# Keeping all row sums for one check at the end, with a second program behind a branch

## The chip, the cores and the metric

The kernel runs on one core of a Trainium2 chip. The metric is the device time of one execution in microseconds. The runs of the kernel before gave 521.4, 522.92 and 527.8 us; their median is 522.92 us.

## The reference

Attention whose heads are mixed before and after the softmax ("talking heads"), followed by a feed-forward block with a squared ReLU. The inputs q, k, v and both mixing matrices are normal draws times 0.1.

```python
batch, n_heads, seq, head_dim = (8, 12, 448, 64)
n_tokens, d_model, d_ff = (3584, 768, 2048)

scores = scale * np.matmul(q, k.transpose(0, 1, 3, 2))        # scale = 1/8
scores = np.einsum('bhij,hg->bgij', scores, w_pre)
scores = scores - np.max(scores, axis=-1, keepdims=True)
attn = np.exp(scores)
attn = attn / (np.sum(attn, axis=-1, keepdims=True) + 1e-09)
attn = np.einsum('bhij,hg->bgij', attn, w_post)
x = np.matmul(attn, v)                                        # to (3584, 768)
h = np.maximum(x @ w_in, 0.0)
out = h * h @ w_out
```

## The kernel before

For each of the 8 batches the 448 queries are cut into 45 chunks of 10 queries (the last has 8), so that 10 queries times 12 heads fill the 128 partitions of a tile, with 4 padding rows in each half. The names of the steps are those of the streams in the code:

- `T` transposes q and k, `QK` (L894) makes the scores of one head, which are copied to `stage` and moved by DMA (`rel`, issued by SyncE, L940) into `dring`, where the 12 heads of a chunk lie side by side on the partitions.
- `pre` (L963) mixes the heads by a matmul. In batch 0 the first 22 chunks go another way (`dir`, L842): there the mix is multiplied into q.
- `exp` (L980, ScalarE) writes the exponential of a chunk to `pring` and, with `accum_out`, its row sums to `rowsum`, a ring of 10 slots. No maximum is subtracted. `rec` (L994, VectorE) takes the reciprocal of the sums of two chunks, and `fold` (L1001, mostly GpSimd) multiplies it into the second mixing matrix, `wk2s`.
- `post` (L1033) mixes the heads again and gives the transposed attention, copied to `a2t` (the `a2ev` tasks, L459 on ScalarE and L460 on VectorE). `AV` (L1092) multiplies by v into `xt`.
- `F1` (L1138, L1159) and `F2` (L1279) are the feed-forward block: ReLU into `h1t` (L1190 on ScalarE, L1191 on VectorE), square into `h2t` (L1200, VectorE), output copied to `osb` and stored, from GpSimd's queue (L1311). The last two tiles of the last batch go through `emit_last` (L1228), and are stored from the queues of SyncE and ScalarE (L1251).

The order of the work is made when the program is built. TensorE's order is written out by hand, in the string `ORDER`, one digit for each unit of a stream. A planner (`_Plan`) walks through it with a cost for every task and puts the tasks of the other engines into lists: each engine runs its list strictly in order and waits on semaphores. Copies out of PSUM carry the engine `FLEX`: the planner gives each to ScalarE or VectorE, whichever would be done earlier by its costs. So a task added on one engine can move a copy to the other one.

```python
def fn_exp(eng, en):                                            # L979
    return eng.activation(pring[:, pr, 0:S], ps[:, gr.banks[x], 0:S], AF.Exp,
                          accum_out=rowsum[:, pr, :])
def fn_rec(eng, en):                                            # L993
    return eng.reciprocal(rinv[:, p0:p0 + n, :], rowsum[:, p0:p0 + n, :])
def fn_final(eng, en):                                          # L1381
    for s in sem_out + [sem_last]:
        eng.wait_ge(s.handle, s.count)
```

At the end SyncE's last task, `final`, waits until all outputs have landed; then every engine branches to a common closing block with a barrier over all five.

Of the kernel before, what the change touches and what calls it, by code (L numbers as in the profile page):

```python
# [7 lines left out]
ALU = mybir.AluOpType  # L8
# [3 lines left out]
PE = "pe"  # L12
# [306 lines left out]
def bass_talking_heads_attention__then__ffn_squared_relu_kernel(  # L319
# [43 lines left out]
    with ExitStack() as es:  # L363
# [14 lines left out]
        WARM = 60000  # L378
        WSHARE = 0.6
# [30 lines left out]
        zrow = sb("zrow", [128, S], DT.bfloat16)  # L410
# [19 lines left out]
        sem_last = Sm("olast")  # L430
        sem_out = [Sm("oslot%d" % i) for i in range(NOS)]

        plan = _Plan(NB)

        def c_pe(t):
            return {PE: (t, t + 190.0)}

        def c_ev(cols):
            return {ACT: (cols / 1.2 + 65.0, cols / 1.2 + 175.0),
                    DVE: (cols / 0.96 + 72.0, cols / 0.96 + 160.0)}  # L440

        def add(name, engine, fn, deps, cost, prio, mode=None, group=None, instrs=0):
            return plan.add(name, engine, fn, deps, cost, prio, "ctr", 1, mode, group=group,
                            instrs=instrs)

        events = {}

        def unit(s, name, fn, deps, ns, mode, group, mms):
            kind = name[:2]
            was = events.get(kind, 0.0)  # L450
            events[kind] = was + EVENTS.get(kind, 0.5)
            n = 2 * mms + int(events[kind]) - int(was)
            t = add(name, PE, fn, deps, c_pe(ns), 0, mode, group, n)
            s.append(t)
            return t

        def copy(eng, en, o, i_):
            if en == ACT:
                return eng.activation(o, i_, AF.Copy)  # L459
            return eng.tensor_copy(o, i_)  # L460

        streams = [[] for _ in range(10)]
        plan.streams = streams
        s_T, s_QK, s_pre, s_post, s_AV, s_dir = streams[:6]
        s_F1, s_F2 = streams[6:8], streams[8:]
# [3 lines left out]
        def fn_init(eng, en):  # L469
            eng.memset(mask[:, :, :], 1.0)  # L470
            eng.memset(wk1[:, :], 0.0)
            eng.memset(wrep[:, :], 0.0)
            eng.memset(wk2b[:, :, :], 0.0)
            return eng.memset(ident[:, :], 0.0)

        t_init = add("init", DVE, fn_init, [], {DVE: (750.0, 850.0)}, -3e6)

        def fn_init2(eng, en):
            return eng.affine_select(ident[:, :], ident[:, :], pattern=[[-1, 128]],
                                     compare_op=ALU.not_equal, fill=1.0, base=0,  # L480
                                     channel_multiplier=1)

        t_init2 = add("init2", POOL, fn_init2, [t_init], {POOL: (310.0, 430.0)}, -1e7 + 1)

        def select(name, m, pattern, base, mult, deps, prio):
            def fn(eng, en):
                return eng.affine_select(m[:, :, :], m[:, :, :], pattern=pattern,
                                         compare_op=ALU.is_ge, fill=0.0, base=base,
                                         channel_multiplier=mult)

            return add(name, POOL, fn, deps, {POOL: (150.0, 250.0)}, prio)

        def halves(name, m, deps, prio):
            def fn(eng, en):
                return eng.tensor_tensor(m[:, 0, :], m[:, 0, :], m[:, 1, :], ALU.add)

            return add(name, DVE, fn, deps, {DVE: (80.0, 160.0)}, prio)

        t_m = select("init3", mask, [[-PR, 2], [-H, H5]], -R0, 1, [t_init], -1e7 + 20)
        t_m = select("init4", mask, [[PR, 2], [H, H5]], R0 + H - 1, -1, [t_m], -1e7 + 21)  # L500
        t_mask = halves("init5", mask, [t_m], -461.0)

        def fn_mask2(eng, en):
            r_ = None
            for x in range(2):
                i_ = ident[64 * x:64 * x + 64, 64 * x:64 * x + PR].rearrange(
                    "p (b a) -> p a b", a=H5)
                r_ = eng.tensor_reduce(mask2[64 * x:64 * x + 64, :], i_, AX.X, ALU.add)
            return r_

        t_mask2 = add("init8", DVE, fn_mask2, [t_init2], {DVE: (330.0, 410.0)}, -460.0)

        def fn_zero(eng, en):
            return eng.memset(vraw[64:128, :, NS - 1, :], 0.0)

        t_zero = [add("zero", DVE, fn_zero, [], {DVE: (300.0, 400.0)}, -3e6 + 1)]
        t_z = []
        t_zrow = add("zrow", DVE, lambda eng, en: eng.memset(zrow[0:R0, :], 0.0), [],
                     {DVE: (300.0, 400.0)}, -3e6 + 2)

        def fn_zdma(eng, en):
            eng.dma_start(dring[0:R0, :, :], zrow[0:R0, :].unsqueeze(1).to_broadcast(
                [R0, NDS, S])).then_inc(sem_z.handle, 16)

        def fn_wsmall(eng, en):
            src = bass.AP(w_pre.tensor, 0, [[0, CH], [H, H], [1, H]])
            eng.dma_start(wrep[R0:R0 + NR, :], src).then_inc(sem_w0.handle, 16)
            for x in range(2):
                src = bass.AP(w_post.tensor, 0, [[H, H], [0, H5], [1, H]])
                eng.dma_start(wrep2[64 * x:64 * x + PR, :], src).then_inc(sem_w0.handle, 16)  # L530
            return None

        def fn_wall(eng, en):
            src = bass.AP(w_pre.tensor, 0, [[0, 128], [1, H * H]])
            eng.dma_start(wall[:, :, :, :].rearrange("p a b c -> p (a b c)"), src).then_inc(
                sem_wq.handle, 16)
            return None

        t_wall = plan.add("wall", SP, fn_wall, [], {SP: (400.0, 5300.0)}, -1e6 - 1, sem_wq, 16)
        wq_of = []  # L540
        for kk in range(2):
            def fn_wq(eng, en, r0=kk * 64, kk=kk):
                r_ = None
                for u in range(2):
                    i_ = wall[r0:r0 + 64, kk:NP:2, u, :].unsqueeze(3).to_broadcast([64, 3, H, H5])
                    r_ = eng.tensor_scalar(wq[r0:r0 + 64, 3 * u:3 * u + 3, :, :], i_,
                                           scale, None, op0=ALU.mult)
                return r_

            wq_of.append(add("wq%d" % kk, DVE, fn_wq, [t_wall], {DVE: (560.0, 640.0)}, -2e6))  # L550

        def fn_wk1(eng, en):
            o = wk1[:, 0:PR].rearrange("p (b a) -> p b a", a=H5)
            i0 = wrep[:, :].unsqueeze(2).to_broadcast([128, H, H5])
            i1 = mask[:, 0, :].unsqueeze(1).to_broadcast([128, H, H5])
            return eng.scalar_tensor_tensor(o, i0, scale, i1, op0=ALU.mult, op1=ALU.mult)

        def fn_wk2(eng, en):
            r_ = None
            for x in range(2):  # L560
                r0, r1 = 64 * x, 64 * x + PR
                i0 = wrep2[r0:r1, :].unsqueeze(2).to_broadcast([PR, H, H5])
                i1 = mask2[r0:r1, :].unsqueeze(1).to_broadcast([PR, H, H5])
                r_ = eng.tensor_tensor(wk2b[r0:r1, :, :], i0, i1, ALU.mult)
            return r_

        t_warm = add("warm", DVE, lambda eng, en: eng.memset(warm[:, :], 0.5), [],
                     {DVE: (600.0, 700.0)}, -4e6)

        def warm_up(gap):  # L570
            now = plan.free[PE]
            if now > WARM or not t_warm.done:
                return
            n = int((gap - 100.0) * (0.42 if now < 6000.0 else WSHARE) / 190.0)
            if n < 1 or plan.find(1, now)[0] > now + gap:
                return
            g = _Group(1)

            def fn(eng, en):
                r_ = None  # L580
                for _ in range(n):
                    r_ = eng.matmul(ps[0:128, g.banks[0], 0:S], warm[:, 0:128], warm[:, :],
                                    start=True, stop=True)
                return r_

            t = add("warm%d" % len(plan.tasks), PE, fn, [t_warm], c_pe(n * 190.0), 0, "full", g,
                    2 * n)
            t.nwait = 0
            g.readers = [[t]]
            start = max(now, t_warm.end + SEM_LAT, plan.find(1, now)[0])  # L590
            plan._commit_pe(t, start + (MODE_SWITCH if plan.mode != "full" else 0.0))

        plan.warm_up = warm_up

# [877 lines left out]
```

## Time and profile before

| what | value |
|---|---|
| runs, us | 521.4, 522.92, 527.8 |
| profiled execution: span, us | 524.4 |
| instructions in the profile | 23175 |
| TensorE (PE) busy | 510.3 us, 97% |
| ScalarE (ACT) busy | 423.3 us, 81% |
| VectorE (DVE) busy | 394.3 us, 75% |
| GpSimd (POOL) busy | 199.1 us, 38% |
| granted TensorE clock, mean | 0.999 |

The span is the time of the profiled execution from its first to its last instruction; the profile gives no other time of its own for this execution. In the profile's rows, `PE ps L1279` means a matmul of line 1279 that writes PSUM; `SPq` and `ACTq` are DMA issues from the queues of SyncE and ScalarE. In a timeline row stand the start, the time and the engine, and in brackets the idle time before with what ended it. In the table of stretches each engine has its busy time and its number of instructions, and after these come the granted clock, the share of DMA and GB/s.

### The profile page before, as it was taken

How to read it: one execution, taken by the hardware profiler on the slowest of the kernel's cores; microseconds unless marked ns; L12 is line 12 of the kernel's file. 1: busy time of each engine (PE TensorE's matmuls, PEld its weight loads, DVE VectorE, ACT ScalarE, POOL GpSimd, SP SyncE). 2: the span in 40 equal slices, each digit the busy share in tenths (PEclk: the TensorE clock that was granted, in tenths of full speed). 3: DMA queues.
4: the chain of work that ended last, by engine and by line, in shares of the span. 5: the costliest groups of instructions: out<-in, count | busy, mean ns of one | idle time of the engine just before them, and what ended most of it. 6: DMA issues, size and time to landing. Idle time of an engine off the chain costs nothing.

```text
span 524.4 us, 23175 instructions
## 1 busy us (share of the span) xinstructions
PE 510.3 (97%) x9633; PEld 322.6 (62%) x9633; DVE 394.3 (75%) x987; ACT 423.3 (81%) x1218; POOL 199.1 (38%) x391
## 2 busy tenths in 40 slices
PE   7999998999999999999999999999999999999997
PEld 4455766567667565566555665566556565567974
DVE  7965978799888669978998769874788678955430
ACT  3788998989989889888997888988888788786411
POOL 9603454423651365135532456124621333132000
PEclk9999999999999999999999999999999999999999
DMA  9999999746984589646984699547974566541003
GB/s 159 199 215 193 153 195 183 185 90 132 172 177 111 121 183 168 144 89 151 174 159 103 139 182 177 113 90 151 175 113 89 118 154 134 115 101 49 2 22 100
DMA packets 82240, 71.85 MB, mean 137 GB/s; under 512 B 13226, under 2 KB 79514, under 8 KB 82138
## 3 DMA queue, kind: packets, MB, share of 16 engines
q0 software_dynamic: 36624, 32.81, 38.4%
q1 hardware_dynamic: 45226, 37.38, 29.6%
q8 instruction: 77, 1.26, 1.0%
q10 hardware_dynamic: 288, 0.20, 0.1%
q14 instruction: 25, 0.20, 0.1%
HBM read 45.70 MB, written 11.01 MB: 108 GB/s over the span
## 4 chain that ended last, share of the span: by engine, by line
PE 87%; DVE 5%; DMA 4%; ACT 1%; issue 1%; POOL 0%; ACTq 0%; POOLq 0%; DVEq 0%
PE ps L1279 26%; PE ps L1159 18%; PE ps L1033 8%; PE ps L963 7%; PE ps L1138 7%; PE ps L1092 7%; PE ps L894 6%; PE ps L842 5%; DMA dring<-stage 3%; DVE stage L460 2%; PE ps L1228 2%; PE ps L745 2%; DMA kraw<-in_k_dram 2%; DVE a2t L460 1%; ACT pring L980 1%
## 5 line engine op out<-in xcount | busy, mean ns | idle before, releaser
L980 ACT ACTIVATE pring<-ps 128x448 bf16<-128x448 f32 x360 | 191.9, 558 | 17.4 <-PE ps L963 8.7
L1279 PE MATMUL ps<-w_out_sb,h2t 64*128 64x384 bf16 x1664 | 151.8, 323 | 0.7 <-issue 0.6
L1001 POOL TENSOR_TENSOR wk2s<-wk2b,rinv 128x120 bf16<-128x120 bf16 (+1 forms) x179 | 70.7, 398 | 198.6 <-DVE rinv L994 197.8
L460 DVE CAST a2t<-ps 128x480 bf16<-128x480 f32 x194 | 118.6, 640 | 18.9 <-PE ps L1033 17.5
L1159 PE MATMUL ps<-xt,w_in_sb 64*128 64x448 bf16 (+2 forms) x1344 | 122.2, 323 | 1.1 <-issue 1.0
L460 DVE CAST stage<-ps 128x448 bf16<-128x448 f32 (+1 forms) x182 | 109.1, 618 | 11.7 <-PE ps L894 7.7
L1279 PEld LDWEIGHTS ps<-w_out_sb,h2t 64*128 64x128 bf16 x1664 | 77.6, 94 | 51.2 <-issue 4.0
L459 ACT ACTIVATE stage<-ps 128x448 bf16<-128x448 f32 (+1 forms) x178 | 92.2, 558 | 20.2 <-PE ps L894 18.0
L459 ACT ACTIVATE a2t<-ps 128x480 bf16<-128x480 f32 (+1 forms) x174 | 92.5, 577 | 12.6 <-PE ps L1033 11.7
L1159 PEld LDWEIGHTS ps<-xt,w_in_sb 64*128 64x128 bf16 x1344 | 61.4, 94 | 41.9 <-issue 2.5
L980 ACT ACTIVATION_READ_ACCUMULATOR pring<-ps 128x1 f32 x360 | 80.1, 222 | 0.0
L1311 POOL DMA_DIRECT2D out_dram<-osb x52 | 33.7, 653 | 111.1 <-ACT pring L980 62.2
L1033 PEld LDWEIGHTS ps<-wk2s,pring 60*128 60x128 bf16 x2880 | 55.9, 93 | 22.1 <-ACT pring L980 2.5
L1033 PE MATMUL ps<-wk2s,pring 60*128 60x60 bf16 x2880 | 62.3, 187 | 0.4 <-POOL wk2s L1001 0.2
L994 DVE RECIPROCAL rinv<-rowsum 128x2 f32<-128x2 f32 (+1 forms) x184 | 29.1, 158 | 37.1 <-ACT pring L980 36.2
L1200 DVE TENSOR_TENSOR h2t<-h1t 128x448 bf16<-128x448 bf16 (+2 forms) x176 | 52.3, 326 | 6.0 <-ACT h1t L1190 5.7
L1190 ACT ACTIVATE h1t<-ps 128x448 bf16<-128x448 f32 (+2 forms) x91 | 40.1, 451 | 20.6 <-PE ps L1159 15.9
L963 PE MATMUL ps<-dring,wk 64*64 64x448 bf16 (+1 forms) x676 | 52.5, 362 | 2.6 <-DVE rinv L994 1.1
L1191 DVE TENSOR_SCALAR h1t<-ps 128x448 bf16<-128x448 f32 (+2 forms) x85 | 41.7, 496 | 17.0 <-PE ps L1159 9.6
L894 PE MATMUL ps<-qkt 64*128 64x448 bf16 (+1 forms) x360 | 49.4, 354 | 0.2 <-DVE qkt L460 0.2
L1138 PE MATMUL ps<-xt,w_in_sb 128*128 128x220 bf16 (+1 forms) x384 | 41.5, 260 | 1.6 <-ACT stage L459 1.6
L1092 PE MATMUL ps<-a2t,vraw 128*64 128x220 bf16 (+1 forms) x768 | 40.4, 260 | 0.2 <-ACT a2t L459 0.2
(57 smaller groups left out, 416.4 us busy)
## 6 DMA issues: line engine op xcount, KB each, us to landing
dring<-stage SPq DMA_DIRECT2D x309, 105.0 KB
out_dram<-osb POOLq DMA_DIRECT2D x52, 192.0 KB, 3.6
qraw<-in_q_dram POOLq DMA_DIRECT2D x42, 112.0 KB, 5.6
kraw<-in_k_dram POOLq DMA_DIRECT2D x42, 112.0 KB, 5.0
w_in_sb<-in_moe_w_in_dram POOLq DMA_DIRECT2D x8, 384.0 KB, 15.0
vraw<-in_v_dram POOLq DMA_DIRECT2D x24, 128.0 KB
w_out_sb<-in_moe_w_out_dram POOLq DMA_DIRECT2D x8, 384.0 KB, 8.2
vraw<-in_v_dram POOLq DMA_DIRECT2D x24, 96.0 KB
```

Source lines behind the costliest of these rows:

```text
L459: return eng.activation(o, i_, AF.Copy)
L460: return eng.tensor_copy(o, i_)
L894: r_ = eng.matmul(ps[y * w:(y + 1) * w, g.banks[x], 0:S], qkt[r0:r0 + 64, pb, p + y, 0, i0:i0 + w], qkt[r0:r0 + 64, pb, p + y, 1, :], star ...
L963: r_ = eng.matmul(ps[64 * y:64 * y + 64, gr.banks[x], 0:S], wk1[64 * x:64 * x + 64 - R0 * x, :], dring[64 * x:64 * x + 64 - R0 * x, (g0 + ...
L980: return eng.activation(pring[:, pr, 0:S], ps[:, gr.banks[x], 0:S], AF.Exp, accum_out=rowsum[:, pr, :])
L1001: return eng.tensor_tensor(wk2s[:, p0:p0 + n, :], i0.to_broadcast([128, n, PR]), rinv[:, p0:p0 + n, :].to_broadcast([128, n, PR]), ALU.mult)
L1033: r_ = eng.matmul(ps[:, gr.banks[x], o0:o0 + PR], pring[64 * x:64 * x + PR, pr + y, j0:j0 + 2 * PJ], wk2s[64 * x:64 * x + PR, pr + y, :], ...
L1092: r_ = eng.matmul(ps[kk * 64:kk * 64 + 64, g.banks[0], x * n:(x + 1) * n], vraw[:, h, s, :], a2t[half][:, s, h, a0:a0 + n], start=(s == 0) ...
L1138: r_ = eng.matmul(ps[:, g.banks[0], 0:n], w_in_sb[:, ft, t * 128:(t + 1) * 128], xt[:, ft, c0:c1], start=(ft == 0), stop=(ft == NFT - 1))
L1159: r_ = eng.matmul(ps[:, g.banks[x], 0:n], w_in_sb[64 * y:64 * y + 64, ft, t * 128:(t + 1) * 128], xt[64 * y:64 * y + 64, ft, c0:c1], start ...
L1200: return eng.tensor_tensor(h2t[:, t16, o0:o0 + n], h1t[:, s, 0:n], h1t[:, s, 0:n], ALU.mult)
L1279: r_ = eng.matmul(ps[:, g.banks[hh], 0:FH], h2t[64 * y:64 * y + 64, t16, col:col + 128], w_out_sb[64 * y:64 * y + 64, t16, hh * FH:(hh + 1 ...
```

## The change

- The ring `rowsum` is replaced by `sums`, which has a place for every chunk of every batch (8 x 46 places). `exp` writes its sums there and `rec` reads them from there. A small filler buffer is cut so that the later buffers keep their alignment, and the row of zeros `zrow` becomes a part of `osb` (the first copies to `osb` wait for the DMA that reads the zeros).
- After all exponentials four VectorE operations take maximum and minimum of all sums on each partition and compare them with 1e30 and 1e-20; a DMA from SyncE (`row`) puts the 128 answers into one row; two VectorE operations reduce them and write an integer, `flag`.
- Everything that builds tasks is put into a function `program(safe)` and called twice, with one set of semaphores that counts on. The second program, `safe`, subtracts the row maximum: for every chunk a maximum and a negation on VectorE, and a bias at the exponential.
- At the end of its list each engine waits for `flag`, loads it into a register and branches: if it is below 1, it runs its part of the second program. SyncE's last task, `final`, stands behind the branch.
- `ORDER` is the same, and serves both programs.

```diff
+        SUM_MOST = 1e30
+        SUM_LEAST = 1e-20
-        rowsum = sb("rowsum", [128, NPS, 1], DT.float32)
+        sums = sb("sums", [128, B * NCP, 1], DT.float32)
+        nmax = sb("nmax", [128, NPS, 2], DT.float32)
+        test = sb("test", [128, 4], DT.float32)
+        flag = sb("flag", [1, 1], DT.int32)
         rinv = sb("rinv", [128, NPS, 1], DT.float32)
-        sb("align", [128, 64], DT.uint8)
+        sb("align", [128, 16], DT.uint8)
...
-        zrow = sb("zrow", [128, S], DT.bfloat16)
+        zrow = osb.bitcast(DT.bfloat16)[:, 0, :, :].rearrange("p a b -> p (a b)")[:, 0:S]
...
+        def program(safe):
...
+            plan.warm_up = None if safe else warm_up
...
+                if safe:
+                    def fn_max(eng, en):
+                        return eng.tensor_reduce(nmax[:, pr, 0:1], ps[:, gr.banks[x], 0:S],
+                                                 AX.X, ALU.max)
+                    def fn_neg(eng, en):
+                        return eng.tensor_scalar(nmax[:, pr, 1:2], nmax[:, pr, 0:1], -1.0, None,
+                                                 op0=ALU.mult)
...
+                    bias = {"bias": nmax[:, pr, 1:2]} if safe else {}
                     return eng.activation(pring[:, pr, 0:S], ps[:, gr.banks[x], 0:S], AF.Exp,
-                                      accum_out=rowsum[:, pr, :])
+                                          accum_out=sums[:, g, :], **bias)
...
-                return eng.reciprocal(rinv[:, p0:p0 + n, :], rowsum[:, p0:p0 + n, :])
+                    return eng.reciprocal(rinv[:, p0:p0 + n, :], sums[:, g0:g0 + n, :])
...
+            def emit_flag():
+                every = [exp_of[b * NCP + c] for b in range(B) for c in range(NCH)]
+                table = sums[:, :, 0].rearrange("p (b c) -> p b c", b=B)[:, :, 0:NCH]
+                def fn_most(eng, en):
+                    return eng.tensor_reduce(test[:, 0:1], table, AX.XY, ALU.max)
+                def fn_least(eng, en):
+                    return eng.tensor_reduce(test[:, 1:2], table, AX.XY, ALU.min)
+                def fn_below(eng, en):
+                    return eng.tensor_scalar(test[:, 2:3], test[:, 0:1], SUM_MOST, None,
+                                             op0=ALU.is_lt)
+                def fn_both(eng, en):
+                    return eng.scalar_tensor_tensor(test[:, 3:4], test[:, 1:2], SUM_LEAST,
+                                                    test[:, 2:3], op0=ALU.is_gt, op1=ALU.mult)
+                def fn_row(eng, en):
+                    eng.dma_start(sums[0:1, 0:128, 0], test[:, 3:4]).then_inc(sem_row.handle, 16)
+                def fn_all(eng, en):
+                    return eng.tensor_reduce(test[0:1, 0:1], sums[0:1, 0:128, 0], AX.X, ALU.min)
+                def fn_flag(eng, en):
+                    return eng.tensor_copy(flag[:, :], test[0:1, 0:1])
+                t = every
+                for n, fn in enumerate((fn_most, fn_least, fn_below, fn_both)):
+                    ns = 480.0 if n < 2 else 80.0
+                    one = add("check%d" % n, DVE, fn, t, {DVE: (ns, ns + 90.0)}, 9e6)
+                    t = t + [one] if n < 2 else [one]
+                t = plan.add("row", SP, fn_row, t, {SP: (1050.0, 2600.0)}, 9e6, sem_row, 16)
+                for fn in (fn_all, fn_flag):
+                    t = add("check%d" % len(plan.tasks), DVE, fn, [t], {DVE: (200.0, 290.0)}, 9e6)
+                return t
...
+        normal, normal_waits, t_flag = program(False)
+        ended = counts()
+        again, again_waits, _ = program(True)
...
         def emit_engine(eng_name, eng):
-            for t in per_engine[eng_name]:
...
+            tasks = normal[eng_name]
+            last = 1 if eng_name == SP else 0
+            emit(eng_name, eng, tasks[:len(tasks) - last], normal_waits)
+            eng.wait_ge(ctr[DVE].handle, t_flag.semval)
+            good = eng.value_load(flag[0:1, 0:1])
+            with eng.If(good < 1):
+                for s_, v_ in ended:
+                    eng.wait_ge(s_.handle, v_)
+                emit(eng_name, eng, again[eng_name], again_waits)
+            emit(eng_name, eng, tasks[len(tasks) - last:], normal_waits)
```

More of the change, by code (lines that the diff above doesn't have):

```diff
@@ L430, in bass_talking_heads_attention__then__ffn_squared_relu_kernel @@
         sem_last = Sm("olast")
+        sem_row = Sm("row")
         sem_out = [Sm("oslot%d" % i) for i in range(NOS)]
[L433 to L444, printed above, removed]
@@ L558, in fn_wk2 @@
[L558 to L568, printed above, removed]
@@ L570, in warm_up @@
[L570 to L579, printed above, removed]
-                r_ = None
-                for _ in range(n):
-                    r_ = eng.matmul(ps[0:128, g.banks[0], 0:S], warm[:, 0:128], warm[:, :],
-                                    start=True, stop=True)
-                return r_
[L586 to L591, printed above, removed]
@@ new lines, in program, with warm_up, fn @@
+            t_warm = add("warm", DVE, lambda eng, en: eng.memset(warm[:, :], 0.5), [],
+                         {DVE: (600.0, 700.0)}, -4e6)
+            def warm_up(gap):
+                now = plan.free[PE]
+                if now > WARM or not t_warm.done:
+                    return
+                n = int((gap - 100.0) * (0.42 if now < 6000.0 else WSHARE) / 190.0)
+                if n < 1 or plan.find(1, now)[0] > now + gap:
+                    return
+                g = _Group(1)
+                def fn(eng, en):
+                    r_ = None
+                    for _ in range(n):
+                        r_ = eng.matmul(ps[0:128, g.banks[0], 0:S], warm[:, 0:128], warm[:, :],
+                                        start=True, stop=True)
+                    return r_
+                t = add("warm%d" % len(plan.tasks), PE, fn, [t_warm], c_pe(n * 190.0), 0, "full", g,
+                        2 * n)
+                t.nwait = 0
+                g.readers = [[t]]
+                start = max(now, t_warm.end + SEM_LAT, plan.find(1, now)[0])
+                plan._commit_pe(t, start + (MODE_SWITCH if plan.mode != "full" else 0.0))
@@ L1087, in fn_av, with emit_post, fn_post @@
+            def emit_post(g0):
+                gs = members(g0)
+                b, c0 = divmod(g0, NCP)
+                half = 0 if c0 < HC[0] else 1
+                n = len(gs)
+                pr = g0 % NPS
+                cs = (c0 - half * HC[0]) * CH
+                nt = min(n * CH, S - c0 * CH) // 2
+                gr = _Group(2)
+                old = [av_of.get((b - 1, half))]
+                def fn_post(eng, en):
                     r_ = None
-                    for x in range(2):
+                    for y in range(n):
@@ new lines, in after_F1, with fn_relu, fn_sq @@
+            def after_F1(b, parts, t16, t_h, c0, n, g, x):
+                s = n_h1["n"] % NH1
+                n_h1["n"] += 1
+                def fn_relu(eng, en):
+                    if en == ACT:
+                        return eng.activation(h1t[:, s, 0:n], ps[:, g.banks[x], 0:n], AF.Relu)
+                    return eng.tensor_scalar(h1t[:, s, 0:n], ps[:, g.banks[x], 0:n], 0.0, None,
+                                             op0=ALU.max)
+                t_r = add("relu%d_%d_%d" % (b, c0, t16), FLEX, fn_relu, [t_h, h1_free.get(s)],
+                          c_ev(n), b * 1000.0 + 600)
+                g.readers[x].append(t_r)
+                o0 = hbase(b) + c0
+                def fn_sq(eng, en):
+                    return eng.tensor_tensor(h2t[:, t16, o0:o0 + n], h1t[:, s, 0:n],
+                                             h1t[:, s, 0:n], ALU.mult)
+                t_s = add("sq%d_%d_%d" % (b, c0, t16), DVE, fn_sq,
+                          [t_r] + [f2_of.get((b - 1, x)) for x in range(4)],
+                          {DVE: (n / 1.92 + 80, n / 1.92 + 160)}, b * 1000.0 + 610)
+                t_s.two = True
+                h1_free[s] = t_s
+                for part in parts:
+                    sq_of.setdefault((b, part), {})[t16] = t_s
@@ new lines, in program @@
+            waits = {}
+            for t in committed:
+                e = t.engine
+                kn = known[e]
+                ws = []
+                for d in sorted((d for d in t.deps if d.sem is not None),
+                                key=lambda d: -d.end):
+                    if e == PE and d.engine == PE and d not in t.sync:
+                        continue
+                    if kn.get(d.sem, 0) >= d.semval:
+                        continue
+                    ws.append((d.sem, d.semval))
+                    for s_, v_ in d.clock.items():
+                        if kn.get(s_, 0) < v_:
+                            kn[s_] = v_
+                waits[t] = ws
+                t.clock = dict(kn)
+                if t.sem is not None:
+                    t.clock[t.sem] = max(t.clock.get(t.sem, 0), t.semval)
@@ new lines, in program, with counts, emit @@
+            return per_engine, waits, t_flag
+        def counts():
+            every = list(ctr.values()) + [
+                sem_w0, sem_hq, sem_z, sem_v, sem_wq, sem_last, sem_row, *sem_dsl, *sem_dsx, *sem_out]
+            for row in sem_qk + sem_w:
+                every += row
+            return [(x, x.count) for x in every if x.count]
+        normal, normal_waits, t_flag = program(False)
+        ended = counts()
+        again, again_waits, _ = program(True)
+        def emit(eng_name, eng, tasks, waits):
+            for t in tasks:
```

1485 lines of the change are left out of this document (730 added, 755 removed).

## The prediction, made before the changed kernel ran

> **What bounds the kernel now.** I read the page first, its busy shares and its chain that ended last, then the table of stretches, then the timeline at the two places that the change touches.
>
> ```profile
> span 524.4 us, 23175 instructions
> PE 510.3 (97%) x9633; PEld 322.6 (62%) x9633; DVE 394.3 (75%) x987; ACT 423.3 (81%) x1218; POOL 199.1 (38%) x391
> PE 87%; DVE 5%; DMA 4%; ACT 1%; issue 1%; POOL 0%; ACTq 0%; POOLq 0%; DVEq 0%
> 10.00:475.00 465.00, 457.33 (x8803) 283.63 (x8803) 372.19 (x913) 405.18 (x1179) 186.03 (x365) 1.00 0.75 147
> 475.00:485.00 10.00, 10.00 (x240) 8.61 (x236) 5.83 (x17) 5.20 (x13) 1.82 (x4) 1.00 0.17 43
> 485.00:521.00 36.00, 35.86 (x500) 26.92 (x494) 9.92 (x35) 9.59 (x24) 2.48 (x4) 1.00 0.15 40
> 521.00:524.40 3.40, 0.00 (x0) 0.00 (x0) 0.00 (x0) 0.38 (x1) 0.00 (x0) 0.88 0.21 58
> ```
>
> TensorE is busy in 510.3 of 524.4 us at the full granted clock (1.00 in the column after POOL's), and the chain runs over it for 87%. So whatever the other engines get or lose counts only if TensorE waits for it, and the most that any rearrangement could win is the 14.1 us in which it idles. Two places remain: the stretch from 475 to 485 us, where TensorE has no gap at all and VectorE is busy for only 5.83 of 10 us, and the last 3.4 us, where no engine computes but ScalarE for 0.38 us.
>
> **The change part by part: the running program.** Laid side by side up to the new branch, the two instruction lists are equal on TensorE and GpSimd. SyncE gets one DMA, `row`, after its last `dring` issue and ahead of the six last output issues. VectorE gets six operations, and one eviction of `a2t` goes from VectorE to ScalarE. The row sums go to another address with the same two instructions (ACTIVATE and its accumulator read), so each exponential costs what it did; the zeros lie in `osb` and are written by the same memset. Buffers behind the sums move by 1,536 bytes, a multiple of 512, so their remainders stay. All this I take as 0.
>
> **The check itself.** It stands behind the last reciprocal:
>
> ```profile
> 474.67 0.45 DVE L994 RECIPROCAL rinv<-rowsum 128x2 f32<-128x2 f32 x2
> 475.62 0.57 ACT L459 ACTIVATE a2t<-ps 128x480 bf16<-128x480 f32 x1 [0.23 <-PE ps L1033]
> 475.62 0.66 DVE L460 CAST a2t<-ps 128x480 bf16<-128x480 f32 x1 [0.50 <-PE ps L1033]
> 478.05 0.35 ACT L1190 ACTIVATE h1t<-ps 128x220 bf16<-128x220 f32 x1 [1.86 <-PE ps L1159]
> 478.84 0.66 DVE L460 CAST a2t<-ps 128x480 bf16<-128x480 f32 x1 [2.56 <-PE ps L1033]
> 480.14 0.56 DVE L460 COPY osb<-ps 128x384 f32<-128x384 f32 x1 [0.64 <-PE ps L1279]
> 481.18 0.38 DVE L1191 TENSOR_SCALAR h1t<-ps 128x220 bf16<-128x220 f32 x1
> 484.61 0.27 DVE L1200 TENSOR_TENSOR h2t<-h1t 128x220 bf16<-128x220 bf16 x1 [0.24 <-ACT h1t L1190]
> 488.19 0.27 DVE L1200 TENSOR_TENSOR h2t<-h1t 128x220 bf16<-128x220 bf16 x1 [3.31 <-ACT h1t L1190]
> ```
>
> The maximum and the minimum each read 360 sums of 128 partitions. No row has that; below stands a reciprocal of two elements at 0.16 us, above the cast of 480 elements at 0.66, and I take 0.5, nearer to the cast by its length. The two comparisons of one element I take at 0.16 us each. From 475.12 that is 2 x 0.5 + 2 x 0.16 = 1.3 us, to 476.4 (between 475.8 and 477.1 at the ends). The eviction that stood there at 475.62 goes to ScalarE right behind its own one, 476.2 to 476.8, 0.5 us later than now; ScalarE was idle there for the 1.86 us before 478.05, which hides it. VectorE's next work comes at 478.84 anyway, so the four operations lie inside its 2.56 us of idle time.
>
> Then `row` goes out at about 476.5, and behind it two more VectorE operations wait for its landing. They stand between the eviction at 478.84 and the one at 480.14. VectorE runs its list in order, so if the row is late, everything behind waits: the `osb` copy, two `a2t` casts, the ReLUs and squares, and through the PSUM banks TensorE. No row moves 4 bytes from each of 128 partitions. The nearest are the transfers of the output:
>
> ```profile
> DMA to landing us min/median/max: 2.2/3.1/5.9
> out_dram<-osb SPq DMA_DIRECT2D x6, 96.0 KB, 2.2
> out_dram<-osb ACTq DMA_DIRECT2D x2, 96.0 KB, 2.5
> out_dram<-osb POOLq DMA_DIRECT2D x52, 192.0 KB, 3.6
> ```
>
> At 3.1 us it lands at 479.6; the eviction ends at 479.50; two operations at 0.16 us end at about 479.9, ahead of 480.14. Cost 0. At 2.2 us it is hidden more deeply. At 5.9 us it lands at 482.4, the copy starts at 482.7 instead of 480.14, and VectorE is 2.6 us late; it has 3.31 us of idle time before 488.19 to make that up, but TensorE could stand for up to 2.6 us before. I take 0 and keep 0 to +2.6. A gain is excluded here, since nothing is taken away from TensorE's work.
>
> **The end.** Each engine now loads the flag from SBUF into a register, compares, and jumps over the second program: behind the branch stand 10,135 entries on TensorE, 1,236 on ScalarE, 1,579 on VectorE, 435 on GpSimd and 427 on SyncE. SyncE alone then waits for the outputs, and all meet at the closing barrier.
>
> ```profile
> 510.28 10.57 PE L1228 MATMUL ps<-w_out_sb,h2t 128*128 128x384 bf16 x64
> 510.39 0.56 DVE L460 COPY osb<-ps 128x384 f32<-128x384 f32 x1 [2.04 <-PE ps L1279]
> 511.44 1.24 POOL L1311 DMA_DIRECT2D out_dram<-osb  x2 [1.36 <-DVE osb L460]
> 514.91 7.10 SPq L1251 DMA_DIRECT2D out_dram<-osb  x6
> 520.89 0.49 ACT L459 ACTIVATE osb<-ps 128x384 f32<-128x384 f32 x1 [2.11 <-PE ps L1228]
> 521.41 0.64 ACTq L1251 DMA_DIRECT2D out_dram<-osb  x1
> ```
>
> The last issue starts at 521.41 and lands 2.5 us later (ACTq's median), at 523.9; 0.5 us of closing is left to 524.4. TensorE ends at 520.85, VectorE at 510.95, GpSimd at 512.68, so they have 3.0, 13 and 11 us of cover. ScalarE and SyncE have only what lies between the end of their own last issue (521.41 + 0.64 = 522.05, and 514.91 + 7.10 = 522.01) and 523.9: 1.9 us. So the price is (load + jump) - 1.9, if positive. The trace before has neither. Below, both are 0 and hidden. Above, each is a transfer as long as the longest output, 5.9: 11.8 - 1.9 = +9.9 us. Code comes in by DMA here:
>
> ```profile
> q8 instruction: 77, 1.26, 1.0%
> q14 instruction: 25, 0.20, 0.1%
> L980 ACT ACTIVATION_READ_ACCUMULATOR pring<-ps 128x1 f32 x360 | 80.1, 222 | 0.0
> ```
>
> Page by page (16 KB and 8 KB, from bytes by packets), in order. A jump of more than 400 instructions leaves such a page, so I price it as one small transfer with nothing else in the queues, 2.2 us. The load of one word has no transfer beside it; between the accumulator read at 0.22 and a 2.2 us transfer I take 1.2. Together 3.4 - 1.9 = +1.5 us.
>
> [...]
>
> **Sum.** 0 in the stream, 0 at the check, +1.5 at the end: the profiled execution goes from 524.4 to 525.9 us. The span takes in everything from the first to the last instruction. The runs without a profile have a median of 522.92 us (521.4 to 527.8), 1.5 below the span, and I carry the difference over: 524.4 us.
>
> **The rivals.**
>
> *The jump costs nothing.* Load and jump stay within the 1.9 us of cover: 522.9 us. For it: nothing has to be fetched if the target is at hand, and the accumulator read shows that a small readout can take 0.22 us. Against it: code is fetched in pages and the target is one or more pages off on every engine.
>
> *Row and jump both at their upper ends (slower).* If `row` takes 5.9 us, VectorE stands in its list and TensorE loses up to 2.6 us; with load and jump at 5.9 us each, another 9.9: 522.9 + 12.5 = 535.4 us, +2.4%. It decides from load and jump together at 12.4 us (1.9 hidden, 10.5 seen), or less with the row's share. For it: VectorE is in order and SyncE and ScalarE have little cover. Against it: 5.9 us is the longest of all output transfers and 3.1 their middle, and the queues are emptier here: the last stretch moves 58 GB/s and the one at 475 moves 43, against 147 between 10 and 475 (last column of the table of stretches).
>
> *The doubled program slows the stream.* If each of the 77 code pages of q8 made TensorE wait 0.15 us more, that is 11.6 us, 534.5 us. For it: twice the code. Against it: the pages up to the branch are the same in number and order, and the transfers take 1.0% of the engines' time.
>
> *The flag says no, and the second program runs.* Then VectorE has its 394.3 us again plus 360 maxima at up to 0.66 (the cast of 480 elements) and 360 negations at 0.16, 690 us, more than TensorE's 510: about 1210 us in all. Against it: scores are products of numbers near 0.1, so each sum is near 448, far from 1e-20 and 1e30, and padding rows give exp(0).
>
> *Faster by over 2%* would take 10.5 of TensorE's 14.1 idle us, and the change removes no wait.
>
> **How the numbers follow.** Forecast 0.64, free jump 0.25, row and jump at their upper ends 0.05, slower stream 0.02, second program 0.02, faster 0.02. Within 2% (10.5 us, about what a measurement of this kernel can tell from no change): 0.64 + 0.25 = 0.89; slower 0.09; faster 0.02. The range starts at the fastest run before with nothing added, 521.4, and ends at the slowest run before plus the forecast's 1.5, 529.3, which also holds load and jump at GpSimd's 3.6 us each (7.2 - 1.9 = 5.3, 528.2); the upper ends beyond it belong to the cases of 0.05 and less.
>
> **What would show it.** Right: TensorE's busy time at 510 and no new entry among its waits; the new VectorE operations between 475 and 480, the `osb` copy still at 480.1; about 3 us between ScalarE's last issue and its barrier, with the span near 526. The check is wrong if the `osb` copy moves by more than 0.5 us or TensorE shows a gap near 481; the end is wrong if the span ends where it did or over 4 us later. Any growth between 10 and 475 us would refute the claim that the stream is untouched.

## The result and the profile after

The changed kernel takes 526.99 us (median of 12 runs, 525.74 to 530.57); the kernel before has 524.70 us over 12 runs. The two medians lie 2.3 us apart. The comparison of all runs gives a ratio of 1.0069 with a 95% interval of 1.0043 to 1.0094, or +3.6 us (2.3 to 4.9). The forecast was 524.4 us, +1.5. The growth is clear of zero and well below the bound of 2%.

The page of the changed kernel, with its second queue of instructions:

```profile
span 524.9 us, 23192 instructions
PE 511.1 (97%) x9633; PEld 322.8 (61%) x9633; DVE 395.1 (75%) x992; ACT 423.7 (81%) x1219; POOL 199.2 (38%) x391
q14 instruction: 33, 0.27, 0.2%
```

Its table of stretches, columns as before:

```profile
10.00:475.00 465.00, 459.81 (x8848) 285.25 (x8845) 373.48 (x917) 406.55 (x1181) 186.65 (x366) 1.00 0.75 147
475.00:485.00 10.00, 10.00 (x236) 8.98 (x230) 5.38 (x17) 5.34 (x13) 1.29 (x2) 1.00 0.18 43
```

TensorE idles 524.9 - 511.1 = 13.8 us, against 14.1 before, and has no gap from 475 to 485. TensorE's end wanders from execution to execution, also with the same kernel, so two spans must not be compared as they are: 520.9 before, here 518.9, and in a second profile of the same changed kernel 521.6. What can be compared is the tail, from the end of ScalarE's last output issue to the end of the span.

The check, in the timeline of the changed kernel, first VectorE, then SyncE's queue and ScalarE:

```profile
472.73 0.46 DVE L1018 RECIPROCAL rinv<-sums 128x2 f32<-128x2 f32 x2
473.10 0.51 DVE L1354 TENSOR_REDUCE test<-sums 128x1 f32<-128x360 f32 x1
473.64 0.53 DVE L1357 TENSOR_REDUCE test<-sums 128x1 f32<-128x360 f32 x1
474.20 0.15 DVE L1360 TENSOR_SCALAR test<-test 128x1 f32<-128x1 f32 x1
474.39 0.16 DVE L1364 SCALAR_TENSOR_TENSOR test<-test 128x1 f32<-128x1 f32 x1
476.90 0.66 DVE L467 CAST a2t<-ps 128x480 bf16<-128x480 f32 x1 [2.35 <-PE ps L1057]
477.47 0.26 DVE L1371 TENSOR_REDUCE test<-sums 1x1 f32<-1x128 f32 x1
477.77 0.14 DVE L1374 CAST flag<-test 1x1 int32<-1x1 f32 x1
478.20 0.56 DVE L467 COPY osb<-ps 128x384 f32<-128x384 f32 x1 [0.29 <-PE ps L1304]
474.58 0.56 SPq L1368 DMA_DIRECT2D sums<-test  x1
473.68 1.04 ACT L466 ACTIVATE a2t<-ps 128x480 bf16<-128x480 f32 x2 [0.23 <-PE ps L1057]
476.11 0.35 ACT L1214 ACTIVATE h1t<-ps 128x220 bf16<-128x220 f32 x1 [1.40 <-PE ps L1183]
```

And the time from issue to landing of the row, from the view of the tile `test`:

```profile
DMA to landing us min/median/max: 2.0/2.0/2.0
```

The row lands 2.0 us after its issue, at 476.6, ahead of the eviction that VectorE does first; the `osb` copy waits for TensorE and not for the check. ScalarE does both evictions in a row and still idles 1.40 us before its next work. All of it is covered. The rest of the stream confirms it: from the start of the last two reciprocals (474.67 before, 472.73 now) to the end of ScalarE's last output issue (522.05 and 520.10) the same 47.4 us pass in both kernels, and the traces of all eleven experiments agree on this distance within 0.01 us. So behind the last reciprocal neither the check nor the moved eviction costs anything; what comes before it wanders.

The end, first from the timeline:

```profile
518.95 0.49 ACT L466 ACTIVATE osb<-ps 128x384 f32<-128x384 f32 x1 [2.11 <-PE ps L1252]
519.47 0.63 ACTq L1276 DMA_DIRECT2D out_dram<-osb  x1
```

Then from the views of the lines of the load (L1513), the branch (L1514) and the closing block (L1520); such rows give the shortest, median and longest duration in ns, then the first and last start:

```profile
L1513 PEldq TENSOR_LOAD <-flag x1: 492/492/492, 515.8 to 515.8; - x1
L1513 SPq TENSOR_LOAD <-flag x1: 995/995/995, 520.1 to 520.1; - x1
L1513 ACTq TENSOR_LOAD <-flag x1: 1121/1121/1121, 520.1 to 520.1; - x1
L1514 PEldq COMPARE_BRANCH  x1: 3435/3435/3435, 516.4 to 516.4; - x1
L1514 SPq COMPARE_BRANCH  x1: 50/50/50, 521.2 to 521.2; - x1
L1514 ACTq COMPARE_BRANCH  x1: 50/50/50, 521.6 to 521.6; - x1
L1520 PEldq DRAIN  x1: 73/73/73, 519.9 to 519.9; - x1
L1520 SPq COMPARE_BRANCH  x1: 43/43/43, 524.0 to 524.0; - x1
L1520 ACTq DRAIN  x1: 66/66/66, 524.6 to 524.6; - x1
```

ScalarE's last issue ends at 519.47 + 0.63 = 520.10. The load takes 1.12 us, the compare begins at 521.6, and the next instruction, the closing drain, begins 3.0 us later, at 524.6; the span ends at 524.9. The tail is 4.8 us. Before, in the closing block's line, ScalarE drained right behind its issue, and SyncE came to the barrier once the outputs had landed:

```profile
L1426 ACTq DRAIN  x1: 619/619/619, 522.1 to 522.1; - x1
L1426 SPq COMPARE_BRANCH  x1: 38/38/38, 524.0 to 524.0; - x1
L1426 SPq DRAIN  x1: 7/7/7, 524.2 to 524.2; - x1
```

That tail was 524.4 - 522.05 = 2.4 us. The tail has grown by 2.4 us, which lies inside the measured 2.3 to 4.9, though near its lower end. TensorE's own load and branch (515.8 to 519.8) start ahead of its last matmuls, which end at 518.9, and it is at the barrier at 519.9.

### The profile page after: what moved, and what is told of

It reads as the page before. It is cut to its first block, busy times and chain, and to the rows that moved or that the text cites. A ratio compares the mean times of both kernels' runs of the same rounds, so it can differ in the third digit from the quotient of the medians.

```text
span 524.9 us, 23192 instructions
## 1 busy us (share of the span) xinstructions
PE 511.1 (97%) x9633; PEld 322.8 (61%) x9633; DVE 395.1 (75%) x992; ACT 423.7 (81%) x1219; POOL 199.2 (38%) x391
## 4 chain that ended last, share of the span: by engine, by line
PE 89%; DMA 4%; DVE 3%; POOL 1%; ACT 1%; issue 1%; SPq 0%; DVEq 0%
PE ps L1304 26%; PE ps L1183 20%; PE ps L1057 8%; PE ps L970 7%; PE ps L1116 7%; PE ps L901 6%; PE ps L1162 5%; PE ps L849 5%; DMA dring<-stage 2%; PE ps L1252 2%; DMA kraw<-in_k_dram 2%; PE ps L752 2%; DVE stage L467 2%; PE ps L589 1%; POOL vraw L654 1%
## 5 line engine op out<-in xcount | busy, mean ns | idle before, releaser
L467 DVE CAST a2t<-ps 128x480 bf16<-128x480 f32 (+1 forms) x193 | 118.0, 640 | 19.8 <-PE ps L1057 18.4
L1018 DVE RECIPROCAL rinv<-sums 128x2 f32<-128x2 f32 (+1 forms) x184 | 29.0, 158 | 36.9 <-ACT pring L1003 36.2
```

## The experiments

Two theories. By the theory of the end, load and code jump behind the last output issue are the whole cost. By the theory of the stream, the check, the row and the moved eviction cost time on the way, or the doubled code does.

| kernel | ratio to before (95%) | tail, us |
|---|---|---|
| changed | 1.0069 (1.0043 to 1.0094) | 4.8 |
| changed, again | 1.0047 (1.0014 to 1.0079) | 5.5 |
| no branch | 0.9999 (0.9974 to 1.0025) | 2.3 |
| short jump | 0.9993 (0.9968 to 1.0018) | 2.3 |
| two loads | 1.0093 (1.0056 to 1.0130) | 7.1 |
| both jump early | 1.0014 (0.9983 to 1.0045) | 2.5 |
| no load | 1.0023 (0.9996 to 1.0050) | 4.6 |
| flag set | 1.0015 (0.9987 to 1.0043) | 4.2 |
| ScalarE jumps early | 1.0014 (0.9988 to 1.0039) | 4.1 |
| four far jumps | 1.0215 (1.0146 to 1.0284) | 13.8 |
| four near jumps | 1.0006 (0.9973 to 1.0038) | 2.3 |

**No branch.**

```diff
-        again, again_waits, _ = program(True)
...
-            good = eng.value_load(flag[0:1, 0:1])
-            with eng.If(good < 1):
-                ...
```

> The changed kernel's sums, its check and its flag stay; the load of the flag, the branch and the second program are left out, so nothing acts on the flag. Tail here means the time from the end of ScalarE's last output issue to the end of the span: 2.4 us before, 4.8 us changed. Theory of the end (load and code jump behind the last output issue make the 0.7%): tail 2.4 us, ratio to before 1.000, within 0.998 to 1.002. Rival, theory of the stream (the check, the row and the moved eviction make it): the ratio stays near 1.007 with a tail of 2.4 us.

The check without its consequence costs nothing that can be measured: 0.9999, tail 2.3 us. Against the changed kernel's 1.0069, whose interval does not touch this one, the theory of the stream falls as far as the check, the row and the eviction go. Against the changed kernel run again (1.0047, 1.0014 to 1.0079) the intervals do overlap; there the tail and the equal 47.4 us decide. The doubled code is left out here too, and is tested below.

**Short jump.**

```diff
             with eng.If(good < 1):
-                for s_, v_ in ended:
-                    eng.wait_ge(s_.handle, v_)
-                emit(eng_name, eng, again[eng_name], again_waits)
+                eng.wait_ge(ctr[DVE].handle, t_flag.semval)
```

> Check, load and branch stay, but behind the branch stands one instruction in place of the second program, so the target is in the same or the next code page; nothing is redone if the flag says no. Theory of the end, with the code fetch as the larger part: load 1.0 to 1.1 us and a compare of 0.05 stay below the 1.9 us of cover, tail 2.4 to 2.6 us, ratio 1.000 to 1.001. If the load alone were the cost, tail and ratio stay at 4.8 us and 1.007. Theory of the stream: 1.007 with a tail of 2.4 us.

0.9993, tail 2.3 us. ScalarE's last issue in its timeline:

```profile
517.35 0.64 ACTq L1276 DMA_DIRECT2D out_dram<-osb  x1
```

Its branch (L1513) and its closing block (L1517):

```profile
L1513 ACTq COMPARE_BRANCH  x1: 50/50/50, 519.4 to 519.4; - x1
L1517 ACTq DRAIN  x1: 8/8/8, 519.6 to 519.6; - x1
L1517 SPq COMPARE_BRANCH  x1: 38/38/38, 519.9 to 519.9; - x1
```

From branch to drain 0.2 us instead of 3.0, and ScalarE is ready ahead of SyncE, which still waits for the outputs. So the load alone is hidden and the far jump is what shows.

**Two loads.**

```diff
+            first = eng.alloc_register("first")
+            eng.reg_load(first, flag[0:1, 0:1])
+            with eng.If_lt(first, 1):
+                eng.wait_ge(ctr[DVE].handle, t_flag.semval)
             good = eng.value_load(flag[0:1, 0:1])
```

> The changed kernel with the flag loaded and compared twice on every engine; the first branch has one instruction behind it. Theory of the end: both loads lie in line ahead of the jump on ScalarE and SyncE, whose cover is used up already, so the tail grows by one load, from 4.8 to about 5.9 us, ratio to before about 1.009. Theory of the stream: nothing moves against the changed kernel, 1.007 and the same tail.

The direction is right, the size missed by 1.2 us. Its loads (L1514, L1517) and its closing block (L1524):

```profile
L1514 ACTq TENSOR_LOAD <-flag x1: 1120/1120/1120, 521.4 to 521.4; - x1
L1517 ACTq TENSOR_LOAD <-flag x1: 291/291/291, 523.0 to 523.0; - x1
L1524 ACTq EVENT_SEMAPHORE  x1: 17/17/17, 526.9 to 526.9; - x1
L1524 SPq EVENT_SEMAPHORE  x1: 17/17/17, 528.5 to 528.5; - x1
```

A second load takes only 0.29 us. Of the 2.3 us by which the tail grows, 1.6 are SyncE, which passes the closing barrier that late after the others. In that gap q14, the instruction queue, brings two pages of code. That a page ends inside the closing block is a guess; no run shows it.

**Both jump early.** Load, branch and jump of ScalarE and SyncE go ahead of the last `osb` copies and output issues:

```diff
+            cut = len(tasks) - last
+            if eng_name in (ACT, SP):
+                cut = min(n for n, t in enumerate(tasks)
+                          if t.name.startswith(("odlast", "oev%d_2" % (B - 1), "oev%d_3" % (B - 1))))
+            tail = tasks[cut:len(tasks) - last]
+            emit(eng_name, eng, tasks[:cut], normal_waits)
...
             with eng.If(good < 1):
+                emit(eng_name, eng, tail, normal_waits)
...
+            if tail:
+                with eng.Else():
+                    emit(eng_name, eng, tail, normal_waits)
```

> The changed kernel with load, branch and jump of ScalarE and SyncE taken ahead of the last four osb copies and the last output issues, which stand behind the branch (and in the other arm ahead of the second program). ScalarE jumps in its 3.5 us gap ahead of those copies, SyncE in its idle time. Theory of the end: the first of these copies comes about 1 us later, with no one behind it in a hurry, the last issue stands where it did, and the tail goes back to 2.4 to 2.9 us; ratio to before 1.000 to 1.002. Theory of the stream, or of the doubled code as such: 1.007 stays.

1.0014 (0.9983 to 1.0045), tail 2.5 us, with the second program still in place. Its loads (L1518) and ScalarE's closing drain (L1529):

```profile
L1518 SPq TENSOR_LOAD <-flag x1: 478/478/478, 477.1 to 477.1; - x1
L1518 ACTq TENSOR_LOAD <-flag x1: 674/674/674, 507.6 to 507.6; - x1
L1529 ACTq DRAIN  x1: 628/628/628, 519.3 to 519.3; - x1
```

ScalarE's work behind the jump, in the timeline:

```profile
511.62 0.49 ACT L466 ACTIVATE osb<-ps 128x384 f32<-128x384 f32 x1 [3.51 <-PE ps L1252]
...
518.64 0.64 ACTq L1276 DMA_DIRECT2D out_dram<-osb  x1
```

The jump fits into ScalarE's gap: the copy behind it still waits for TensorE and is not late by the 1 us that was expected (its idle time before is 3.51 us without the jump too). By the tail this excludes the doubled code as such; the ratio alone, with an interval up to 1.0045, would not. It is the version to keep: the guard is there, and no cost shows. No run here executes the second program.

**The changed kernel again, no load, flag set, ScalarE alone.** One chip, beside each other. The first is unchanged.

> The changed kernel once more, beside the kernel before and the next three on one chip, as their yardstick. Tail as before: from the end of ScalarE's last output issue to the end of the span. Theory of the end: tail 4.8 us against 2.4 before, so a ratio near 1.005 (2.4 us of 523) and not over 1.007. Rival: besides the tail the stream itself costs about 1 us (1.007 was 3.6 us, the tail grew by 2.4), then 1.007 stays.

1.0047, near the 1.005 of the tail alone; its interval (1.0014 to 1.0079) does not exclude 1.007. Its tail is longer than the first one's because ScalarE's jump takes 3.8 us here.

```diff
-            good = eng.value_load(flag[0:1, 0:1])
-            with eng.If(good < 1):
+            good = eng.alloc_register("good")
+            eng.reg_mov(good, 1)
+            with eng.If_lt(good, 1):
```

> The changed kernel with the load of the flag left out: each engine puts the constant 1 into a register and branches on that, so the flag is not acted on; the jump over the second program stays. Theory of the end: ScalarE's 1.1 us of load and 0.3 us up to the compare fall away, the jump of 3.0 us stays, so the tail goes from 4.8 to about 3.5 us, ratio near 1.002 to 1.003. If the load were all, 2.4 us and 1.000; if only the jump counted and the load were hidden, 4.8 us and no change against the changed kernel.

The ratio came as expected, 1.0023, the tail did not. Its branch (L1515) and its closing drain (L1521):

```profile
L1515 ACTq COMPARE_BRANCH  x1: 50/50/50, 522.5 to 522.5; - x1
L1521 ACTq DRAIN  x1: 67/67/67, 526.5 to 526.5; - x1
```

The load is gone, and the compare begins 0.4 us after the last issue's end (522.1) instead of 1.5. But this execution's jump took 3.9 us, so the tail is 4.6 us where 3.5 was expected. Taken alone it is near the 4.8 us of a hidden load; beside the changed kernel with a like jump (3.8 us, tail 5.5) it is 0.9 us shorter, so the load does count once the cover is used up.

```diff
-                def fn_most(eng, en):
...
+                t = add("flag", DVE, lambda eng, en: eng.memset(flag[:, :], 1), every,
+                        {DVE: (80.0, 170.0)}, 9e6)
```

> The changed kernel without the check: the six operations and the row's DMA are left out, and one memset on VectorE at the same place sets the flag to 1. Load, branch and jump stay. Theory of the end: tail 4.8 us and the same ratio as the changed kernel beside it, within 0.2%. Rival, the check costs in the stream: the ratio falls by 0.2% or more with the same tail.

1.0015, 0.3% under the changed kernel beside it, more than the 0.2% that were allowed; but the intervals overlap, the tail is shorter as well (4.2 us; ScalarE's jump took 2.7), and the version without a branch, which has the check, stands at 0.9999. By the ratio it is inconclusive; but without the check the same 47.4 us pass from the last reciprocals to ScalarE's last issue, so the check costs nothing there.

The fourth has the edit of the early jumps with `(ACT,)` in place of `(ACT, SP)`.

> As the version with both early jumps, but ScalarE alone jumps early; SyncE loads and jumps behind its last output issue as in the changed kernel. Theory of the end: both engines are late by nearly the same, SyncE by 0.5 us less than ScalarE in the changed profile, so taking ScalarE out alone wins only about 0.4 us: tail about 4.3 us, ratio near 1.004 to 1.006. If ScalarE alone held the end, the tail falls to 2.4 to 2.9 us and the ratio to 1.000 to 1.001.

The closing drain of ScalarE and the closing branch of SyncE, which comes behind its jump and the outputs:

```profile
L1529 ACTq DRAIN  x1: 621/621/621, 518.5 to 518.5; - x1
L1529 SPq COMPARE_BRANCH  x1: 43/43/43, 522.2 to 522.2; - x1
```

The tail of 4.1 us is near the 4.3 expected: SyncE alone holds the end nearly as late, so both engines have to jump early. The ratio of 1.0014 is below the 1.004 expected; ratios of this width do not resolve 1.5 us, the tail does.

**Four jumps in a row.** To lift the cost out of the scatter, the second program is replaced by four branches on ScalarE and SyncE, over 300 instructions each (for `size` 600 the built program has 300 wait instructions), or over one.

```diff
-            with eng.If(good < 1):
...
+            for size in (600, 600, 600, 600) if eng_name in (ACT, SP) else (2,):
+                with eng.If(good < 1):
+                    for _ in range(size):
+                        eng.wait_ge(ctr[DVE].handle, t_flag.semval)
```

> The changed kernel without the second program. Behind the load, ScalarE and SyncE take four branches in a row, each over 300 wait instructions that would return at once; the other engines take one, over one instruction. Nothing is redone if the flag says no. Theory of the page fetch: each of the four jumps stalls its engine for about 3.0 us (2.6 to 3.9 in the runs so far), so the tail is 1.4 us of load + 12 of jumps + 0.3 = 13.7 us (12 to 17) against 2.4 before: ratio about 1.021 (1.018 to 1.028). Rival, the stall is paid once (a wait for the outputs or for the first page, whatever the number of jumps): tail 4.8 to 5.5 us, ratio 1.003 to 1.007.

> As the version with four jumps over 300 instructions, but each over one. Theory of the page fetch: a branch whose target is in the page costs 0.05 us and its decode, so four add at most 0.7 us to a load that has 0.5 us of cover left; tail 2.3 to 2.9 us, ratio 1.000 to 1.001. Rival, a taken branch stalls by itself: as with 300 instructions, a tail over 12 us.

1.0215 against 1.0006, and tails of 13.8 us (13.7 expected) and 2.3. The page of the far version, then the row of its instruction queue in the near one:

```profile
span 533.2 us, 23198 instructions
...
q14 instruction: 41, 0.34, 0.2%
```

```profile
q14 instruction: 26, 0.21, 0.1%
```

The branches of the far version, then of the near one, by their line:

```profile
L1514 ACTq COMPARE_BRANCH  x4: 45/45/50, 520.9 to 529.9; - x4
```

```profile
L1514 ACTq COMPARE_BRANCH  x4: 45/45/50, 523.0 to 523.4; - x4
```

Four far branches begin (529.9 - 520.9) / 3 = 3.0 us apart, four near ones 0.15, with 45 ns for the branch itself. The cost is paid for each jump, and q14 brings 41 pages of code against 26: 15 more for eight far jumps, about two for each.

**A ladder of lengths.** The same with sizes of 40, 80, 160, 240, 320, 480, 800 and 1600 waits, in one execution.

> Eight branches in a row on ScalarE and SyncE, over 20, 40, 80, 120, 160, 240, 400 and 800 wait instructions; the second program is left out, and nothing is redone if the flag says no. Theory of the page fetch, with 8 KB pages of 128 instructions (bytes by packets of the instruction queue) and the next page at hand: bodies of 20, 40 and 80 cost under 0.3 us each, those of 240, 400 and 800 about 3 us each whatever their length, 120 and 160 one or the other by where the page ends; four to five stalls, a tail of 14 to 18 us. Rival, the cost grows with the length: the body of 800 takes twice that of 400.

The trace's records of the branch instructions give the time from each branch to the next instruction of its engine:

| instructions jumped | 20 | 40 | 80 | 120 | 160 | 240 | 400 | 800 |
|---|---|---|---|---|---|---|---|---|
| ScalarE, us | 0.17 | 0.15 | 2.08 | 2.30 | 2.14 | 3.07 | 3.02 | 3.02 |
| SyncE, us | 0.18 | 0.50 | 0.17 | 2.06 | 2.08 | 3.11 | 3.00 | 2.93 |

The cost doesn't grow with the length; it has three steps. The shortest jumps cost 0.2 us (one of them 0.5, which stays open), those from 240 instructions on 3.0, and between them stands 2.1, which was not expected. ScalarE's jump over 80 was forecast under 0.3 us and cost 2.1. That the next page is at hand, on which this forecast stood, was assumed and is not shown. The 128 instructions of a page are an estimate: before the change q8 and q14 brought 1.26 + 0.20 = 1.46 MB for 23175 instructions, 63 bytes each. The tail is 17.7 us, within the 14 to 18 expected, but from six stalls on ScalarE instead of four to five. The instruction queue tells the steps apart. From 520.2 to 522.19 us each of the two engines stands in one stall of 2.1 us, and from 529.75 to 532.7 the code for one stall of 3.0 comes in for each; q14 in these two windows:

```profile
q14 instruction: 2, 0.02, 2.9%
q14 instruction: 4, 0.03, 4.2%
```

So in the ladder a stall of 2.1 us goes with one 8 KB page and one of 3.0 with two, which the trace has directly after one another. The whole execution agrees: five stalls with one page and six with two make 17, and q14 brings 43 pages against the 26 of the version with four near jumps. This count is no general rule: in the changed kernel VectorE jumps at 509.2 and GpSimd at 510.5, they go on 3.0 and 2.6 us later, and by VectorE's next instruction, at 512.3, q14 has brought only two pages for both. That code is fetched in the stall is shown; why a far target takes a second page in the ladder is not.

## Why the prediction was right

- **The stream at 0.** Right: the check without branch stands at 0.9999 (0.9974 to 1.0025), and TensorE's busy time at 511.1 us against 510.3. Its busy time between 10 and 475 us did grow, from 457.33 to 459.81, which the prediction named as a refutation; but 8848 matmuls lie in this stretch instead of 8803, because this execution reached them 1.9 us earlier.
- **The check at 0, with the `osb` copy on time.** Right in its parts: 0.51 and 0.53 us for the reductions (0.5 forecast), 0.15 and 0.16 for the comparisons (0.16), 0.26 and 0.14 behind the row (0.16 each), and 2.0 us for the row, for which 3.1 was taken within 2.2 to 5.9: just below the lower end. The `osb` copy moved from 480.14 to 478.20, more than the 0.5 us that were to refute the term, but the last reciprocals moved by the same 1.94 us. One figure of the working is off: at its upper prices the four operations end at 476.8, not 477.1; nothing else uses it.
- **The end at +1.5 us.** Right in mechanism, too small in size: the tail grew by 2.4. The cover held: 1.9 us forecast, and before the change SyncE's closing branch stood at 524.0, 2.0 us after 522.05. The load was near, 1.1 us against 1.2, which was luck, since 1.2 was the middle between two rows of other kinds; 0.3 us until the compare was left out. The mis-sized term is the jump, priced as a small transfer of 2.2 us: 3.0 on ScalarE, 2.7 to 3.9 in the profiles with the same jump at the end. The transfer of a page is the smaller part of it: the DMA records of the ladder give 0.3 to 0.6 us for a page. The sum by the measured terms is 1.1 + 0.3 + 3.0 - 1.9 = 2.5, less 0.1 for a shorter closing (0.3 us instead of 0.4). From ScalarE's last issue to its barrier it was 4.5 us, not about 3.
- **Profile to time.** The 1.5 us between span and median came from three runs; over twelve the median before is 524.7. Runs lie 1.8 us above their own span before and after, so the term cancels in the difference. The absolute 524.4 was low by 2.6 us: 1.8 by the median of only three runs, the rest by the jump. It lies below the 524.70 of the kernel before, and the range of 521.4 to 529.3 holds no change as well; that the measured time falls into it says little, the parts of the tail say more. The span was to be near 526 and was 524.9, because TensorE's end came 1.9 us earlier in this execution.
- **The rivals.** The free jump is what the short jump shows, not the change, whose interval starts at 1.0043. Upper ends: the row took 2.0 us, the load 1.1 and the jump at most 3.9, all far from 5.9, and four far jumps were needed to come to about 2%. The slower stream and the second program did not occur.

## What to carry to other kernels

Price a branch over much code at about 3 us per jump and engine, as it cost here (2.93 to 3.11 us from 240 instructions on in the ladder, 2.7 to 3.9 on ScalarE over the second program), and look for the engine that has the least time between its own last issue and the landing of the last output: there it is paid; here VectorE and GpSimd, with 10 us or more, hid it. Put load and branch of that engine into an earlier gap and its last tasks behind them; then a guard with a whole second program behind it costs nothing that shows, as here (1.0014, tail 2.5 us). Where the scatter of the runs (here over 1%) is larger than the effect, measure the tail in the trace, or multiply the suspect.

## What the runs showed of the hardware

- Jump cost in steps in the ladder: 0.15 to 0.18 us (once 0.50), 2.06 to 2.30 and 2.93 to 3.11. It did not grow with the length from 240 instructions to 800, and over 80 it was 2.08 on ScalarE and 0.17 on SyncE. Code is fetched in the stall: in the ladder one 8 KB page in 2.1 us and two in 3.0. Behind the last issue, over the second program, ScalarE's jump took 2.7 to 3.9.
- Loading one word from SBUF into a register took 0.49 us on TensorE and GpSimd, 0.7 on VectorE, 1.0 on SyncE and 1.1 on ScalarE right behind a DMA issue, but 0.48 and 0.67 there when nothing had just been issued, and 0.28 to 0.33 for a second load at once on all but GpSimd, where it took 0.84.
- TensorE's sequencer took load and branch ahead of its queued matmuls (load at 515.8 us, last matmul's end at 518.9), so its jump of 3.4 us was hidden.
